# Attention with a SwiGLU gate on one core: projection steps in the issue table, rows by a task list, last phase by query blocks

## The chip, the core and the metric

The kernel runs on one core of a Trainium2 chip. The metric is the time of one execution on the device, in microseconds; a kernel's figure is the median of its runs.

## What is computed

x is 2048 x 512. It is layer-normalised, goes through full softmax attention with 32 heads of 16 columns and an output projection, and through a SwiGLU feed-forward of width 1792 whose result, passed through silu, scales the attention output. All of it is fp32.

```python
qkv = xn @ wqkv                       # S=2048, D=512, H=32, Dh=16
p = softmax(q @ k.T * Dh ** -0.5)     # per head
s = (p @ v).reshape(S, D) @ wo
h = silu(xn @ w1) * (xn @ w3)
g = silu(h @ w2)
return x + s * g
```

## The kernel before

Products that need fp32 accuracy run in the fp32r format with each operand split into a high and a low part; `split3` does a product as three matmuls (low x high, high x low, high x high). The values product is a plain fp32 matmul.

A prologue normalises x, transposes it, makes the values (`vt`, with a column of ones behind each head's 16), and writes q and k to DRAM. Then 32 *phases* run: 16 pairs of heads (`p`), each with the queries in two halves of 1024 (`half`). A phase has three kinds of steps:

- 64 *maxima* (m): a 62-row matmul of queries by keys into a PSUM bank (L482), whose row maxima DVE takes (L484). After the 64, `max_rows` makes them negative, transposes them (L496) and writes them by four small DMAs (L507) into two rows of the phase's `qs` tile, so that the scores come out with the maximum subtracted.
- 64 *scores* (s): keys by queries with 64 rows (L514); ACT takes the exponential into a `pt` tile (L517; there are 13).
- 16 *value blocks* (v): for a chunk of 128 keys, four fp32 matmuls of `vt` and four `pt` tiles (two heads, two blocks of 512 queries) side by side into one accumulator, `pv` (L524). The ones give the sums of the exponentials.

After the last value block of a phase `take_out` copies `pv` to `ot` (L530), writes the sums by DMA to a narrow tile (L536), takes 16-column reciprocals (L538), goes through DRAM to spread them over the rows (L540, L543), multiplies (L545), splits on POOL (L548, L549) and writes eight row pieces, `o<-oh` and `o<-ol` (L557), to DRAM. For the last pair, half 0, they go straight into the projection's tiles.

Beside the phases runs the feed-forward (f, L737), in blocks of 512 tokens in the order 3, 0, 1, 2, each in two halves of the width; its result g goes to DRAM, block by block. Weights arrive by DMA in `wr` and POOL splits them (L285, L286).

Scores, maxima and feed-forward matmuls use 64 of PE's 128 rows. Two such steps run at a time, one in each half, which the code calls lanes. The order in which everything is issued on PE is a string, `ORDER_OF_ISSUE`: f, m and s are steps of the lower lane, F, M and S of the upper, v is a value block, R the second part of `max_rows` (r: that and a value block), a dot an idle slot of the planner. A small planner (`Model`, with planned times of the lanes, ACT, DVE, POOL and DMA) runs along while the instructions are emitted. It decides which PSUM bank is taken and when the small steps of `max_rows` and `take_out` are put in; a step that can't go yet by its plan is put in `late` and emitted at the next place where it can. On the chip each engine and each DMA queue runs its instructions in the order of emission, held by semaphores.

The string covers 488 of the 512 value blocks. For the rest, a loop chooses steps by the planner's state. The output projection has 16 tiles of 128 tokens x 512, each twelve matmuls (`project`, lines L187, L189, L191 with the tile named `o`), and a `finish` on DVE: times g, plus x (L783, L785). It needs the attention rows (`ov`, fetched by L821), the output weights (L832, split on DVE at L825 and L826) and x and g (`bring`, L775, L776). All these DMAs are issued on SP, the fetches and `bring` from `open_chunk` at fixed chunk counts after the feed-forward's end. The loop takes six projection matmuls at a time when a counter (`beside["due"]`) says so.

Tokens of blocks 2 and 3 get their projection without the last two heads; these follow after the last value block. The closing chain there copies `pv`, transposes it, takes reciprocals, spreads and transposes back, multiplies, splits, and does a small projection of 64 rows for each tile of blocks 2 and 3 with a `finish` each (L1083 to L1114).

Of the kernel before, what the change touches and what calls it, by code (L numbers as in the profile page):

```python
# [26 lines left out]
VW = DH + 1  # L27
ORDER = (3, 0, 1, 2)
# [4 lines left out]
FEND = 3  # L33
RATE = 6
SPARE = 12
# [11 lines left out]
    "mMmMmMmM.fMffMffMffMffMffMfM.fMfm.Mm.MffFFffFfFFfFffFfFfFmFFmFffMfMfMffFFfFffFFmFfFfmFFmFmfFFffMfMfm"  # L47
    "MffMfmFfFfFfFFmFfFfmFFmFmFFfMffMfFffFFfFffFFmFfFfmMmFFmfFFmm.Mmf.MffMffFFfFffFFfFmFmFfFmfFFfFffMm.Mm"
    "MmFFffFfFfFfFfFfFfFfFmFfFfMfMfMmMmFfFfFfFfFFffFfFFffFFRFfMffMMfmFFfFfmFFmFfmFFfFmFfFfmFmMffSfMfmFfFf"
    "FfFfFFffFFffFFmfFSfmFfMfSffMfSfFfFfFmFsFmFfFsFmMfFsFfFfFfMfMfSfMfMfsFFffFFsFmFfmFmFSfFfFmFmvsMfMsFvv"  # L50
    "mSfSFfmSFffFsMfFsFmFsFFfMfSffSmFFffSmFfMvSmsMFmvFsMsMfFsfFFfMfsFfFMfSsfFMffMFfsFMfFfsFmFmSvvmSFsmFsF"
    "mFvSmfFSmfSFffMSffFmSfFmFsFfFmFSfSfmMvsMsMsMvsMMsfSMfvsMfMfSfMfMfSMfrvsMMffMfSfSffSfMsFffFsFFmsFfSmF"
    "fFfSmFmFFfSmvsMsMvvMsFffSFfmFFsSfmFfFfSfMfFFsFmfFSsmFvSsMffMsMvSmSfsFfMfFFfsMfFsFMfSffFMsfFFsmFfSFfm"
    "MvSmmMvSmmFsFFfFfsFmFSfFsmFfFfSMfFmFfmSvsMSmMfMfvSfmMMsvvSmfFsFfFFsMfmSfFsFfFmFfSMfFfmSvsMmSmFvSmmFF"
    "sfSfFfFMsfFMfMfsFFfMsfFfSfFsFMfsFfMSfmRvSmmSMmvvSfMffSfFsMFfsFmFsFFfmFsFmFmFsFFffSfMFfmSFfmFsFFfFmsF"
    "mFmFvSmmFsSvvMffSMffSfSFfMffSFfmSFfsFmFsFFfmFsFsFmFMfvvSmsSmMvsMSsFmFmvSmsFmFFmFsSsvmSfMSffSFffMsFFf"
    "sMfFMfSfMffFmSfFMmvSmmSmFvsFmFFmFsFsFmfFFsFffMfSSfMfSfFfMfMffFMmvsMMfMsvvSmSmFfmFfFFsmFFsSffFmFMfsFM"
    "ffSfFsFsFMfmrsMmSfMMfvsSfMmSvmSmMMsvsFfFSfmFSfFfMsFfSfMffSfFmFsFFmsFMffFFmMfSmvvMfSsFsFmfFfFmFsFfFmS"
    "fFSfMfsFfFsMfFMfMfsFvSsmSsSvvmSMfMsvSfMsFffFfSmFfSFsFmfFfFFsfSMffFFsfFMfFmmMvvSmfFFsmFFsFfMsFfFsmFSf"
    "FfmSFfSfSfMfFfmMFfvsMmSsSvvMsfMvMsSmSffFFfFfFsFmFfFsFmfSMfSffFmFSffFfMFmvvsMfSMfSffFfFfSMfsFMfFsFfFm"  # L60
    "sFFsFsmFFsFRvmSfSfMfMvsMSmmSvFmSmsSmFvSmsFmFfSfFfFFmfFsSMffFSffMFfMfMfsFfFsSvvMsMfsFsFFfFfFmFsFsFmSf"
    "FfmFmFFfmSvSmSssMvvmSMffSfSfMfMfSfSffMsMfFfsFsFfFmFmFMsvsMfMfSfFSffFmFsFMfmFmFvSmSmFmvSsmFMmvsMfSfMF"
    "fsFfFfMsFFfmSFfFsmFfSfFMmfFSffMvsMMfsSvsMsMMfvvsMfMfSSffSfMfMfMsrsMfMSfFffSFfMfSffMFfsFFsmFmFvvmSSfm"
    "SFfFfFfmFsFFfmSfFsFMfSfFfMsfFFmfFsFFfsSvsMSmmFvvSffMSfMfSffFfMsFsFFmmFFfSffMfFSmvsMsFmFsFfFFmsFFfMsf"
    "FsFMfsFFfmSFfMfSfmFvvSfSmSsMfvMsfMMfvSmmFsFsFFfFfMsfFsFMfsFfFSmFfFmSffFmFmSvSmsFsFmFFffFMsFfmFSfMfFf"
    "MsvvSsSfMfMffSfMvsMMmSrSmFssFFsFmmFvmSmFFsFffSFfmSmFSfFmfFsFFmFfFsFmFsFmfFfSFmSmvvSmSfSffMfSvMfsSfSm"
    "FFfFfFsFmFfFsMfsFfFsMfFsFMfMfFfmMvSmMfMmvvSmfSsFmFFfFfSmFfFsFmfFFsFmsFFmMfvsMMsSmvSmfSMffMfMfSMfvSfM"
    "ffMfMSffMfFFsFfFfsFmFmSFfFfsFsFMfsFFmMvMsmFsSvSmmSmMvsMSmvSmSffMfFsFFfMsfFSfSfFfMfMffSfFFsFmFmsFsFmF"
    "rMsFmmMFsvsMSmmFvSmSmFffFSfFfSfMfsFfFMfSfMfSffFFmFmmSmvvmFsFFssFFmFfMfsFFfmFsFmFfFSfMfMfSfmSvSmMsSsv"
    "sMSfMfMfMfvSmmMvSmsFfFFsFmFfsFMfFfsFMfFsfMFsfFMffMSffMMfvSmmSvSmSmmFvmMsFsFFsFfFfsFmFFfmSfFSffFmSfFS"  # L70
    "fMfMffFsSvMsSfMmvsMMfmFfFFsfFfSmFfFSfFmfSFmFfsFmFmFvMsmMMsvvsMfSMffSMfrSmfMSfsFfFFmsFFfMsfFFsMffMFfs"
    "FfMMfsFfFfFsSvMsSsmFmFvSmMsSmvfMfSmSfFfFfSmFsFfFMfSffFmSfFFsfFMfFfmMvvSsfSmMvmSFfsMsFFffSMfFfsFmFsFf"
    "FmFsFFfMfSfSfmMvsMMmmFvvSmFssFmFfFFfsFMfFsfMsFFfSfmSfsMffFfFmSfSfFmMvvmSmSvmSfFsFFmFsFfFmsFfMSfFfSfm"
    "FSffFMsfFMfsFMfvsMsMMsvsMSfSffMMffMfMrvsMfSfMMffSfMfSfSffSfFmFFfFmFsFmFfsMFfMsvSmmSFmvvMsFfFfFsSmFfF"
    "sFsfFMfFffSmFSffFSfMfFsFfSsvvmSSmSmvSmFmsFsFFmFsFmFmFsFmvsMmFsFFsFfFfMsfFSfMfSffFmFFsfMfFSffMfMfFFsM"
    "mvSsMsfSvmMSmMfvvSmSfSfMffSfMfMvsMfSmMFffFfFsFfFSsfFmFFsfFsFmFFfmMvsMsFfSfMfFfFmSFfSfMfSfFfmSFffFmFs"
    "FfMRvsMmMsSvvSmSffMvMsSmmFfFFffFSfFsFmFfsFFsFmfFSfmFFsfFmFFsmFFmSfFfFmFmSfvSmmMSmvmFFsFssMvSssMmFFmv"
    "vSfMffSfSMffFSfmFsFFfsMfFsFMfMfFfmMvvmMSffMFffSfFfSfMfSfMFfsMfFfMsFFmFFsFmmFFsFFsvMsmFmSSvSmSmmSvSmF"
    "ssFmFfFFfMsfFFsMffFFsMsFfMfMfvMsSfMfsSvMsMfMsfMvSffSMfSfmFFsFfFmsFFfmSfFsFFmmFFfFmSfSfRvSmsMMmvvSfMf"
# [61 lines left out]
def kernel(ctx: ExitStack, tc: tile.TileContext, x, wqkv, wo, w1, w3, w2, out):  # L141
# [1000 lines left out]
```

## Time and profile before

| | |
|---|---|
| time, median of 3 runs | 1836.4 us (1832.53 to 1837.69) |
| profiled execution | 1835.77 us, span 1834.0 us |
| granted TensorE clock, mean | 0.985 |
| PE busy | 1785.8 us (97%), 13120 matmul records |
| DVE busy | 1478.9 us (81%) |
| ACT busy | 1241.7 us (68%) |
| POOL busy | 692.0 us (38%) |
| DMA | 147.27 MB, mean 80 GB/s |

PE is the engine that matmuls run on, PEld its weight loads, which overlap. PE is counted as busy while a started matmul waits or runs at a low clock, so 97% does not say how near it is to its best. Times in the profile count from the start of the span. A line of the timeline has a start, a length, the engine, the line, the output and input tiles; in brackets, how long the engine was idle before it and what ended that. SPq is the queue of SP.

### The profile page before, as it was taken

The numbers are of one execution on the slowest core, as the hardware profiler recorded it, in microseconds if no ns is written. First come the engines' busy times: TensorE is split into PE (matmuls) and PEld (weight loads), VectorE is DVE, ScalarE is ACT, GpSimd is POOL, SyncE is SP. The second block draws the span as 40 slices with busy tenths as digits, with TensorE's granted clock in tenths as the row PEclk, the third lists the DMA queues.
The fourth block names the chain that finished last, engine by engine and source line by source line (L and its number), as shares of the span: only waits on it lengthen the run. The fifth ranks groups of instructions, "written<-read, shape, count | busy, mean of one in ns | idle before, by whom it ended". The sixth has DMA issues, their size and how long they took to land.

```text
span 1834.0 us, 35315 instructions
## 1 busy us (share of the span) xinstructions
PE 1785.8 (97%) x13120; PEld 1046.2 (57%) x13120; DVE 1478.9 (81%) x2450; ACT 1241.7 (68%) x2357; POOL 692.0 (38%) x720
## 2 busy tenths in 40 slices
PE   7999999999999999999999999999999999999896
PEld 5887655555555555555555555555555555554435
DVE  6425989988899888888888888998888898888415
ACT  3221477777777777777777776877777777777370
POOL 2104832455145514553345414560545235430001
PEclk9999999999999999999999999999999999999898
DMA  6656112122231303122312122132312131201823
GB/s 229 224 176 171 56 41 51 51 55 66 82 85 48 76 25 77 53 60 92 85 47 64 47 48 55 44 76 75 93 48 65 36 77 39 62 16 48 264 67 138
DMA packets 130203, 147.27 MB, mean 80 GB/s; under 512 B 28016, under 2 KB 86384, under 8 KB 126960
## 3 DMA queue, kind: packets, MB, share of 16 engines
q1 hardware_dynamic: 129456, 143.98, 28.6%
q8 instruction: 103, 1.69, 0.4%
q10 hardware_dynamic: 576, 1.05, 0.2%
q14 instruction: 68, 0.56, 0.1%
HBM read 104.33 MB, written 39.58 MB: 78 GB/s over the span
## 4 chain that ended last, share of the span: by engine, by line
PE 87%; DVE 5%; DMA 5%; SPq 1%; issue 1%; POOL 0%; ACT 0%; POOLq 0%; DVEq 0%
PE pv L524 25%; PE f L737 24%; PE e L514 17%; PE m L482 13%; DVE mp L484 4%; PE e L187 1%; PE e L191 1%; PE e L189 1%; DMA qk<-sl 1%; DMA ovl<-o 1%; PE o L187 1%; PE o L189 1%; PE o L191 1%; PE m L187 1%; PE m L191 1%
## 5 line engine op out<-in xcount | busy, mean ns | idle before, releaser
L484 DVE TENSOR_REDUCE mp<-m 128x1 f32<-128x512 f32 x2048 | 1297.6, 685 | 179.7 <-PE m L482 94.4
L517 ACT ACTIVATE pt<-e 128x512 f32<-128x512 f32 x2048 | 1085.5, 615 | 344.3 <-PE m L482 172.6
L482 PE MATMUL m<-ks,qs 62*128 62x512 f32 x2048 | 729.2, 421 | 10.0 <-DVE mp L484 4.9
L514 PE MATMUL e<-qs,ks 64*128 64x512 f32 x2048 | 728.3, 421 | 10.5 <-DVE mp L484 6.7
L524 PE MATMUL pv<-pt,vt 128*17 128x512 f32 x4096 | 523.8, 601 | 0.0
L514 PEld LDWEIGHTS e<-qs,ks 64*128 64x128 f32 x2048 | 343.3, 186 | 300.3 <-ACT pt L517 121.1
L482 PEld LDWEIGHTS m<-ks,qs 62*128 62x128 f32 x2048 | 347.2, 186 | 161.7 <-DVE mp L484 56.4
L737 PE MATMUL f<-xth,wl 64*128 64x512 f32 x896 | 312.5, 398 | 0.8 <-POOL wl L286 0.6
L737 PE MATMUL f<-xth,wh 64*128 64x512 f32 x896 | 309.6, 394 | 0.0
L737 PE MATMUL f<-xtl,wh 64*128 64x512 f32 x896 | 304.7, 394 | 0.0
L737 PE MATMUL f<-wh,hs 64*128 64x512 f32 x896 | 256.3, 394 | 0.0
L286 POOL TENSOR_TENSOR wl<-wr,wh 128x512 fp32r<-128x512 f32 x168 | 217.3, 1293 | 14.0
L285 POOL TENSOR_SCALAR wh<-wr 128x512 fp32r<-128x512 f32 x168 | 104.3, 621 | 260.4 <-DMA wr<-in_B_w_dram 71.5
L524 PEld LDWEIGHTS pv<-pt,vt 128*17 128x17 f32 x4096 | 80.2, 96 | 191.8 <-issue 182.5
L737 PEld LDWEIGHTS f<-xth,wl 64*128 64x128 f32 x896 | 154.8, 186 | 16.2 <-issue 2.1
L737 PEld LDWEIGHTS f<-xth,wh 64*128 64x128 f32 x896 | 156.4, 186 | 11.3
L737 PEld LDWEIGHTS f<-xtl,wh 64*128 64x128 f32 x896 | 153.4, 186 | 11.1
L737 PE MATMUL f<-wl,hs 64*128 64x512 f32 x448 | 156.3, 393 | 0.0
L737 PEld LDWEIGHTS f<-wh,hs 64*128 64x128 f32 x896 | 147.2, 185 | 11.3 <-issue 0.9
L548 POOL TENSOR_SCALAR oh<-ot 128x512 fp32r<-128x512 f32 x31 | 19.3, 621 | 319.5 <-DVE ot L545 319.5
L623 POOL TENSOR_TENSOR h<-g,h 128x512 f32<-128x512 f32 x56 | 72.0, 1285 | 176.0 <-ACT h L619 175.9
L607 POOL TENSOR_SCALAR th<-th 128x512 f32<-128x512 f32 x56 | 34.8, 621 | 156.5 <-ACT th L600 156.5
(112 smaller groups left out, 1219.6 us busy)
## 6 DMA issues: line engine op xcount, KB each, us to landing
wr<-in_B_w_dram SPq DMA_DIRECT2D x168, 256.0 KB
qs<-qk SPq DMA_DIRECT2D x192, 64.0 KB
ks<-qk SPq DMA_DIRECT2D x96, 128.0 KB
qk<-sh SPq DMA_DIRECT2D x32, 256.0 KB
qk<-sl SPq DMA_DIRECT2D x32, 256.0 KB
xin<-in_A_x_dram SPq DMA_DIRECT2D x16, 256.0 KB
g<-part SPq DMA_DIRECT2D x16, 256.0 KB
rb<-rd SPq DMA_DIRECT2D x124, 32.0 KB
```

What stands on the lines that cost most here:

```text
L187: nc.tensor.matmul(ps, lhs[1], rhs[0], start=first, stop=False)
L189: nc.tensor.matmul(ps, lhs[0], rhs[1], start=False, stop=False)
L191: nc.tensor.matmul(ps, lhs[0], rhs[0], start=False, stop=last)
L285: nc.gpsimd.tensor_scalar(hi, t, 1.0, 1.0, op0=ALU.mult, op1=ALU.mult)
L286: nc.gpsimd.tensor_sub(lo, t, raw(hi))
L482: nc.tensor.matmul(ps, qs[p % 2][64 * h:64 * h + KM, q0:q0 + P], ks[p % 2][64 * h:64 * h + KM, c * 512:(c + 1) * 512], start=True, stop=True)
L484: nc.vector.reduce_max(mp[p, half][:, h, qt, c:c + 1], ps, axis=AX.X)
L514: nc.tensor.matmul(ps, ks[p % 2][64 * h:64 * h + KR, k * P:(k + 1) * P], qs[p % 2][64 * h:64 * h + KR, q0:q0 + 512], start=True, stop=True)
L517: nc.scalar.activation(pt, ps, AF.Exp, scale=DH ** -0.5)
L524: nc.tensor.matmul(pv[32 * j:32 * j + VW, :], vt[:, k, 2 * p + j % 2, :], pt, start=(k == 0), stop=(k == NT - 1))
L623: nc.gpsimd.tensor_mul(h2, g, h2)
L737: nc.tensor.matmul(ps, left[r], right[r], start=starts and lane == 0, stop=ends and lane == 1)
```

## The change

The string is replaced by one that covers all 512 value blocks and has 21 letters o, one for each projection step; an o that can't go by the plan goes to `late`. Its other letters are re-laid too. It ends with:

```
old  ...RvvSsSssMvMsMffMfMSffMfSvvmFSmmSFmSmFFsFsFFmFsFsFmFFsFsSsFFmFmFmFFmFmFSvSmSsvSsSmSvSsSmSvMmSssSvSmsMsMvMsMsMvvM
new  ...FSvSsSsSvvMsMsMsSvMsSsSsvMsSsSovsSSssSovsSSsvmSsSSvvvRSssSsSovsSSsSsovsSsSSsovsSsSsSvSsSvosSSsSsvvsSsSsovvSsSsSos
     SsooovSssSsSoovSsSvvvoooooSsSsosSsSooSssSsvsSSvvv....
```

A step o is a whole tile of twelve matmuls at once (order of the blocks: 3, 2, 0), then "sum", then four "last" tiles of block 2, then block 1. The last phase takes its two blocks of 512 queries in turn, all 16 key chunks for block 2 and then for block 3. A value block then holds two key chunks of two heads, so block 2's sums, reciprocals and last product are done while block 3 is being attended; only block 3's are left for the closing chain. The sums are picked and spread by one matmul with a 0/1 matrix (`picks`), and the reciprocal is taken of all 512 columns.

`open_chunk` no longer starts transfers. A list of tasks, each with a condition, is gone through at each letter (`tend`): rows (r), output weights (wr), their split (w, on POOL now), side rows x and g (s), for blocks 3, 2, 0, 1. Nothing is started while the planned DMA work reaches over 3 us ahead. Block 3's rows and the output weights may come before the feed-forward's end. Side rows of block 0 go into the tiles of block 3's rows, those of block 1 into block 2's.

The first part of `max_rows` is put in as soon as its maxima are emitted.

```diff
+        if (p, half) == LAST:
+            qb, k = divmod(k * 2 + qb, NT)
...
-    def values(p, k, pts):
+    def values(p, half, k, pts):
+
+        last = (p, half) == LAST
         for j, pt in enumerate(pts):
-            nc.tensor.matmul(pv[32 * j:32 * j + VW, :], vt[:, k, 2 * p + j % 2, :], pt,
-                             start=(k == 0), stop=(k == NT - 1))
+            key = k * 2 % NT + j // 2 if last else k
+            nc.tensor.matmul(pv[32 * j:32 * j + VW, :], vt[:, key, 2 * p + j % 2, :], pt,
+                             start=key < 2 if last else k == 0, stop=key >= NT - 2 if last else k == NT - 1)
...
+    def split_rows(hi, lo, w):
+        nc.gpsimd.tensor_scalar(hi, w, 1.0, 1.0, op0=ALU.mult, op1=ALU.mult)
+        nc.gpsimd.tensor_sub(lo, w, raw(hi))
...
+    def bring(b):
+
+        if b == 3:
+            xs = [w_raw().rearrange("p a b -> p (a b)") for _ in range(4)]
+            gs = [raw(qs[NP % 2])[:, i * 512:(i + 1) * 512] for i in range(4)]
+        elif b == 2:
+            xs = parts_of(tail.tile([P, KC, 512], F32, name="x2"))
+            gs = [raw(w_split("hl"[i % 2])) for i in range(4)]
+        else:
+            pool, tag = (keep, "xt{}") if b == 0 else (tail, "ov{}2")
+            xs, gs = (parts_of(pool.tile([P, KC, 512], F32, tag=tag.format(v), name=f"in{v}{b}", bufs=1)) for v in "hl")
+        for t in range(4):
+            r = b * 512 + t * P
+            nc.sync.dma_start(xs[t], x[r:r + P, :])
+            nc.sync.dma_start(gs[t], g_d[b][t * P:(t + 1) * P, :])
+            side[b, t] = xs[t], gs[t]
...
+    def weights_split():
+        return wts.split == len(wts.units)
+
+    def attended():
+        return count["S"] >= 64 * (PHASES - 2)
+
+    tasks = [
+        ("r3", lambda: len(lanes.ended) >= 18 * TB * HF - 4, lambda: rows_of(3, by_rows(xt_pair(keep))), 0.0),
+        *(("r3", lambda: 3 in ov, lambda k=k: fetch(3, k), 2.5) for k in range(KC - 1)),
+        ("wr", weights_split, load_output_weights, 5.0),
+        *(("w", lambda: 3 in ov and to_split and attended() and mod.free["pool"] <= mod.now + 0.5,
+           lambda k=k: split_output_weights(k), 0.0) for k in range(KC)),
+        ("s3", lambda: attended() and len(wos) == 2 and len(wos[1]) == KC, lambda: bring(3), 9.0),
+        ("r3", lambda: 3 in ov and taken_out(PHASES - 3), lambda: fetch(3, 3), 2.0),
+        ("open", lambda: state["n"] >= UNITS and not owed, open_tail, 0.0),
+        *(("r2", lambda: tail, lambda k=k: fetch(2, k), 2.5) for k in range(KC - 1)),
+        ("r2", lambda: tail and taken_out(PHASES - 3), lambda: fetch(2, 3), 2.0),
+        ("s2", lambda: tail and len(wos) == 2 and len(wos[1]) == KC, lambda: bring(2), 9.0),
+        *(("r0", lambda: tail, lambda k=k: fetch(0, k), 2.5) for k in range(KC - 1)),
+        ("r0", lambda: tail and taken_out(PHASES - 4), lambda: fetch(0, 3), 2.0),
+        ("r1", lambda: tail and (2, 0) in side, lambda: rows_of(1, [[w_split(v) for _ in range(KC)] for v in "hl"]), 0.0),
+        *(("r1", lambda: 1 in ov, lambda k=k: fetch(1, k), 2.5) for k in range(KC)),
+        ("wl", lambda: 1 in ov, last_rows, 1.0),
+        ("s0", lambda: gone(3), lambda: bring(0), 9.0),
+        ("s1", lambda: gone(2), lambda: bring(1), 9.0),
+    ]
+
+    def tend():
+
+        while tasks and mod.free["dma"] <= mod.now + 3.0:
+            e = next((e for e in tasks if e[1]()), None)
+            if e is None:
+                return
+            tasks.remove(e)
+            e[2]()
+            if e[3]:
+                there[e[0]] = mod.work("dma", mod.now, e[3]) + 2.5
+
+    def got(*names):
+        return not any(e[0] in names for e in tasks) and all(there.get(n, 0.0) <= mod.now for n in names)
+
+
+    steps = [("whole", b, t) for b in (3, 2, 0) for t in range(4)]
+    steps += [("sum", 2, 0)] + [("last", 2, t) for t in range(4)] + [("whole", 1, t) for t in range(4)]
+
+    def can(what, b):
+        if what == "sum":
+            return len(sums) == 2 and sums[1] <= mod.now
+        if what == "last":
+            return len(sums) == 3 and sums[2] <= mod.now and got("wl")
+        return got("w", f"r{b}", f"s{b}") and (b >= TB // 2 or taken_out(PHASES - 2))
...
+    def finish(b, t, i, ps, to, adder=None):
+
+        xr, gr = side[b, t]
+        res = tail.tile([P, 512], F32, tag="res", name="res", bufs=2) if adder is None else pt_tile(F32)
+        nc.vector.scalar_tensor_tensor(res, gr, 0.25, ps, op0=ALU.mult, op1=ALU.mult)
+        (adder or nc.vector).tensor_add(xr, res, xr)
+        free_at[i] = mod.work("dve", max(mod.lane) + 0.25, 1.4) - 0.7
+        if to is not None:
+            r = b * 512 + t * P
+            to.dma_start(out[r:r + P, :], xr)
...
+        if not steps or min(free_at) > mod.now + EARLY or not can(*steps[0][:2]):
+            return False
+        what, b, t = steps.pop(0)
+        i, ps = take("o")
+        if what == "sum":
+            mod.block(4, was_free[i])
+            ot = sums[0]
+            nc.tensor.matmul(ps, picks(), ot, start=True, stop=True)
+            oh, ol = (work.tile([P, 512], F32R, tag=f"o{v}", name=f"o{v}", bufs=1) for v in "hl")
+            nc.vector.reciprocal(rb, ps)
+            nc.vector.tensor_mul(ot, ot, rb)
+            nc.vector.tensor_scalar(oh, ot, 1.0, 1.0, op0=ALU.mult, op1=ALU.mult)
+            nc.vector.tensor_sub(ol, ot, raw(oh))
+            free_at[i] = mod.work("dve", max(mod.lane) + 0.25, 2.0) - 1.2
+            sums.append(free_at[i] + 2.2)
+            side["split"] = oh, ol
+            return True
+        if what == "whole":
+            mod.block(3 * KC, was_free[i])
+            for k in range(KC):
+                run(split3(ps, [v[k][:, t * P:(t + 1) * P] for v in ov[b]], [w[k] for w in wos], k == 0, k == KC - 1))
+        else:
+            mod.block(3, was_free[i])
+            run(split3(ps, [v[:, t * P:(t + 1) * P] for v in side["split"]], wlast, True, True))
+        finish(b, t, i, ps, nc.sync if b < TB // 2 or what == "last" else None)
...
+    def picks():
+
+        if not chosen:
+            m = work.tile([P, P], F32, tag="mh", name="picks", bufs=2)
+            for j in range(4):
+                of = [ident[:, n:n + 1].to_broadcast([P, 32]) for n in (32 * (j % 2) + DH, 32 * (j % 2) + 64 + DH)]
+                nc.vector.tensor_add(m[:, 32 * j:32 * j + 32], *of)
+            chosen.append(m)
+        return chosen[0]
...
-        if tail is None and state["n"] >= UNITS and not owed:
-            open_tail()
-            end = count["chunks"]
-        n = count["chunks"] - end
-        if tail:
-            if n == 1:
-                output_weights()
-                mod.work("dma", mod.now, 4.0)
...
-        if tail and count["V"] < PHASES * NT:
-            beside["due"] = min(beside["due"] + max(beside["left"] - SPARE, 0) / (PHASES * NT - count["V"]), 5 * RATE)
-        if k == NT - 1 and (p, half) != (NP - 1, 1):
+        if (p, half) == LAST:
+            if k == NT // 2 - 1:
+                sums.append(work.tile([P, 512], F32, tag="ot", name="ot", bufs=1))
+                nc.scalar.copy(sums[0], pv)
+                pv_free = mod.work("act", begins + mod.VALUES + 0.3, 0.6) + mod.NOTICE
+                sums.append(pv_free)
+        elif k == NT - 1:
...
-    while count["V"] < PHASES * NT:
+    while count["V"] < PHASES * NT or len(steps) > 1:
         settle()
         small()
-        catch_up()
+        tend()
         if rows and rows[0][2] == 1 and rows[0][0] <= mod.now:
             second()
-        if values_ready(mod.now) and (len(closed) > 1 or not exponentials(0) or not exponentials(1)):
-            issue_v()
-            continue
...
         if values_ready(mod.now):
             issue_v()
...
+        elif not any(half_issued(what, h) for h in sorted(range(2), key=lambda h: mod.lane[h]) for what in "smf"):
+            if not projecting():
+                mod.wait(0.1)
+
+    ot, oh, ol = pt_tile(F32), pt_tile(F32R), pt_tile(F32R)
     nc.scalar.copy(ot, pv)
-    while beside["left"]:
+    while steps:
+        settle()
+        small()
+        tend()
         mod.wait(0.1)
-        small()
         projecting()
-    turned, back = bank("o"), bank("o")
-    for c in range(4):
-        nc.tensor.transpose(turned[:, c * P:(c + 1) * P], ot[:, c * P:(c + 1) * P], ident)
...
+    total = bank("o")
+    for c in (slice(0, 256), slice(256, 512)):
+        nc.tensor.matmul(total[:, c], picks(), ot[:, c], start=True, stop=True)
+    for c in (slice(0, 256), slice(256, 512)):
+        nc.vector.reciprocal(rb[:, c], total[:, c])
+        nc.vector.tensor_mul(ot[:, c], ot[:, c], rb[:, c])
+        nc.vector.tensor_scalar(oh[:, c], ot[:, c], 1.0, 1.0, op0=ALU.mult, op1=ALU.mult)
+        nc.vector.tensor_sub(ol[:, c], ot[:, c], raw(oh[:, c]))
     for t in range(4):
```

More of the change, by code (lines that the diff above doesn't have):

```diff
@@ L27 @@
 VW = DH + 1
+LAST = (NP - 1, 1)
 ORDER = (3, 0, 1, 2)
@@ L836, in output_weights, with split_output_weights, last_rows @@
+    def split_output_weights(k):
+        if not wos:
+            wos.append([raw(ks[NP % 2]).bitcast(F32R)[:, i * 512:(i + 1) * 512] for i in range(KC)])
+            wos.append([])
+        wos[1].append(w_split("hl"[k % 2]))
+        split_rows(wos[0][k], wos[1][k], to_split[k])
+    wlast = []
+    def last_rows():
+        w = tail.tile([P, 512], F32, tag="res", name="res", bufs=2)
         nc.gpsimd.memset(w, 0.0)
@@ L1094 @@
-    spread = tail.tile([P, 512], F32, tag="res", name="res", bufs=2)
-    nc.vector.tensor_copy(spread.rearrange("p (a b) -> p a b", b=32),
-                          rec.rearrange("p (a b) -> p a b", b=1).to_broadcast([P, 16, 32]))
-    for c in range(4):
-        nc.tensor.transpose(back[:, c * P:(c + 1) * P], spread[:, c * P:(c + 1) * P], ident)
-    nc.vector.tensor_mul(ot, ot, back)
-    oh = work.tile([P, 512], F32R, tag="oh", name="oh", bufs=1)
-    ol = work.tile([P, 512], F32R, tag="ol", name="ol", bufs=1)
```

355 lines of the change are left out of this document (136 added, 219 removed).

## The prediction

> **What bounds the kernel now.** I read the busy time by stretches first, with cuts where the character of the work changes: end of the prologue, last feed-forward matmul, first score of the last phase, last value block, last full projection. Columns are length, then busy time of PE, weight load, DVE, ACT, POOL, then granted clock, DMA share and GB/s.
>
> ```profile
> 161.00:1686.60 1525.60, 1515.89 (x11858) 862.64 (x11860) 1350.55 (x2233) 1138.34 (x2161) 657.56 (x674) 1.00 0.24 59
> 1686.60:1746.60 60.00, 50.34 (x244) 23.13 (x245) 29.97 (x53) 27.60 (x55) 4.50 (x7) 0.85 0.70 224
> 1746.60:1780.50 33.90, 33.88 (x198) 11.24 (x199) 2.07 (x3) 31.08 (x63) 1.91 (x2) 0.91 0.12 33
> 1780.50:1813.20 32.70, 32.70 (x144) 26.99 (x145) 15.18 (x22) 0.59 (x1) 0.00 (x0) 1.00 0.50 175
> 1813.20:1834.00 20.80, 5.60 (x33) 3.96 (x31) 13.13 (x19) 0.00 (x0) 5.06 (x4) 0.69 0.32 122
> ```
>
> The first stretch is TensorE at full clock with 9.7 us idle in 1525.6 (1525.60 less 1515.89): nothing but the amount of matmul work counts there. The other four are the tail, 147.4 us, and each has another limit. The first of them holds 244 matmul records in 60 us, where 32.7 us of the fourth hold 144: PE is busy there only because matmuls wait. The chain of waits, cut to the tail, says for what (start, length, piece):
>
> ```profile
> 1692.42 2.87 DMA wr<-in_A_wo_dram
> 1701.47 5.06 DMA ovl<-o
> 1724.11 6.61 DMA wl<-g
> 1730.74 6.56 DMA wl<-o
> 1737.32 3.37 DMA sums<-ot
> 1744.72 1.75 DMA qs<-ml
> ```
>
> From 1692 to 1746 it is a row of transfers: the output weights, attention rows and side rows queued together on SP, and behind them the 2 KB sums and the maxima rows `qs<-ml` that the last phase's scores need. The third stretch is paced by ACT, with projections hardly beside it; the fourth is 12 projection tiles with ACT empty; the fifth is the closing chain. So work of three limits runs in turn, and could in part run side by side. The timeline gives the unit prices and two of the stalls:
>
> ```profile
> 1684.88 0.40 PE L737 MATMUL f<-wh,hs 64*128 64x512 f32 x1
> 1702.43 0.79 PE L514 MATMUL e<-qs,ks 64*128 64x512 f32 x1 [5.97 <-DVE mp L484]
> 1700.00:1705.00 5.00, 2.57 (x12) 0.90 (x16) 4.34 (x8) 1.19 (x2) 0.65 (x2) 0.50 0.88 298
> 1745.26 0.47 PE L514 MATMUL e<-qs,ks 64*128 64x512 f32 x1 [2.52 <-DMA qs<-ml]
> 1753.80 0.66 PE e L514 x4
> 1754.46 0.98 PE pv L524 x8
> 1757.69 19.34 ACT L517 ACTIVATE pt<-e 128x512 f32<-128x512 f32 x39
> 1791.44 0.39 PE L187 MATMUL o<-ks,xtl 128*128 128x512 f32 x1
> 1802.32 0.39 PE L187 MATMUL o<-ks,wl 128*128 128x512 f32 x1
> ```
>
> The last feed-forward matmul ends at 1685.3. Four scores cost PE 0.66 us and a value block 0.98 us where ACT doesn't hold them; an exponential costs ACT 19.34/39 = 0.496 us, so a chunk takes 1.64 us of PE and 1.98 of ACT. A projection matmul takes (1802.32 - 1791.44)/48 = 0.2267 us, a tile of twelve 2.72 us. A wait of 5.97 us left the clock at 0.50 in the stretch 1700 to 1705.
>
> **The body of the table.** The whole string is replaced, so I counted it. Up to value block 450 the old one has 3780 f, 1896 m and 1803 s letters, the new one 3779, 1895 and 1809; adding the larger of the two lanes between value blocks gives 3774 slots against 3780. The work is the same and in the same proportions, so I take no change. Bounds: the 9.7 us of idle could vanish or double, so 9.7 us either way. Up to the last f, the new string has 24 slots (24 x 0.2267 = 5.4 us) and 3 value blocks (3 x 0.98 = 2.9 us) more. They are no extra work, they are only done before that mark: it moves from 1685.3 to 1693.6.
>
> **After the last f.** The string still has 105 scores, 29 value blocks, 6 maxima and all 21 projection steps. On PE: scores 105/4 x 0.66 = 17.3; value blocks 29 x 0.98 = 28.4; maxima 3 slots, 0.7; 16 whole tiles x 2.72 = 43.5; four "last" tiles x 3 x 0.2267 = 2.7; the new sum, one fp32 matmul of 512 columns, about 1.0 by the fp32 value block (0.5 to 2). Sum 93.6 us. ACT needs 105 x 0.496 = 52.1 us beside it, so with projections between the chunks ACT no longer sets the pace. That takes the third stretch's pacing and the fourth stretch's solo run away; what it costs if that cover fails is 0.34 us (1.98 - 1.64) for each chunk without projection beside it, 8 us for 24.
>
> **Transfers.** Bytes stay the same (rows, side rows, weights, 4 MB of output). What moves is their order: rows of block 3 and the output weights come about four down-products before the last f, where the DMA share was low; the rest in batches, each held back until the planned queue is short. The weights' split goes from DVE to POOL, with these prices, four times:
>
> ```profile
> L286 POOL TENSOR_TENSOR wl<-wr,wh 128x512 fp32r<-128x512 f32 x168 | 217.3, 1293 | 14.0
> L285 POOL TENSOR_SCALAR wh<-wr 128x512 fp32r<-128x512 f32 x168 | 104.3, 621 | 260.4 <-DMA wr<-in_B_w_dram 71.5
> ```
>
> 4 x 1.9 = 7.7 us on POOL, which was busy 4.50 of 60 us there; DVE is rid of the block that made the 5.97 us wait. I cost it at nothing; if POOL were late the first projection would wait, up to those 7.7 us.
>
> Each projection now stands in PE's in-order queue at a fixed place. If its rows are late, every score and value block behind it waits too, and ACT and DVE with them. Three places matter, priced by the following rows:
>
> ```profile
> 1631.64 0.59 ACT L530 COPY ot<-pv 128x512 f32<-128x512 f32 x1 [1.80 <-PE pv L524]
> 1656.14 0.42 SPq L557 DMA_DIRECT2D o<-ol  x1
> 1742.55 0.70 SPq L507 DMA_DIRECT2D qs<-mh  x1
> 1746.62 3.21 PE e L514 x9
> SPq L775 <- PE o L191: 29.7, 2, 20.4
> ```
>
> An output of a phase takes 1656.14 - 1631.64 = 24.5 us from the copy to the last row write, plus landing, about 2 us (`qs<-ml` above: 1.75). (1) The first tile needs phase 29's rows; from value block 480 to the first o the string has 44 slots and 8 value blocks, 18 us. Late by 0 to 9; I take 3, since a step that can't go yet is put behind later chunks. (2) The last phase's maxima rows: 4 us from issue to use (1742.55 to 1746.62), behind a transpose and two casts of about 1.2; between it and the last phase's first score stand 8 scores, one tile and one value block, 5.0 us. With side rows queued ahead, one stream of 5.06 us more. 0 to 6, I take 3. (3) Block 0 needs phase 30's rows, written straight into its tiles: 26 us, against seven value blocks (6.9), 35 scores (5.8) and four tiles (10.9), 23.6 us. Late by 2; with block 1's side rows in front, another stream or two: 0 to 12, I take 5. The clock after such waits, by the 0.50 row, about 2. Together 13 us, 2 to 29.
>
> **The closing chain.** Before, it took 20.8 us (fifth stretch). Two rounds of transposes go; one matmul picks the sums, the reciprocal runs over 512 columns instead of 16, in halves.
>
> ```profile
> 1733.93 0.17 DVE L492 TENSOR_SCALAR nm<-mx 128x16 f32<-128x16 f32 x1
> 1814.74 0.25 DVE L1092 RECIPROCAL rec<-o 128x16 f32<-128x16 f32 x1
> 1780.65 0.59 ACT L1083 COPY ot<-pv 128x512 f32<-128x512 f32 x1 [1.66 <-issue]
> 1816.27 0.69 DVE L1099 TENSOR_TENSOR ot<-ot,o 128x512 f32<-128x512 f32 x1 [0.82 <-PE o L1098]
> 1816.99 0.43 DVE L1102 TENSOR_SCALAR oh<-ot 128x512 fp32r<-128x512 f32 x1
> 1819.88 0.69 DVE L783 SCALAR_TENSOR_TENSOR res<-qs,o 128x512 f32<-128x512 f32 x1 [1.73 <-PE o L191]
> 1822.52 1.27 DVE L785 TENSOR_TENSOR wr<-res,wr 128x512 f32<-128x512 f32 x1
> 1830.73 0.34 ACTq L788 DMA_DIRECT2D out_dram<-wl  x1
> ```
>
> Copy with its wait 0.8, first half of the matmul 0.5, four DVE steps over 512 columns 0.69 + 0.69 + 0.43 + 0.69 = 2.5, DVE's four products and two additions 6 x 0.69 = 4.1, one addition slowed beside POOL (1.27) 0.6, first products on PE 0.7, last issue to the end of the span 3.3 (1834.0 - 1830.73): 12.5 us. Block 2's product and half of the additions are already gone, which is where 8 us go. The reciprocal is the unknown: at the multiply's rate it is 0.69; by the two 16-column rows it costs (0.25 - 0.17)/16 = 5 ns a column more, 2.6 us over 512. I take 0.69, as part of the 0.08 us may be a fixed cost; the other end adds 2.6 us at the close, and a little at the first sum, which has value blocks behind it.
>
> **Sum.** 1693.6 + 93.6 + 13 + 12.5 = 1812.7 us of span, 21.3 less than 1834.0. The profiled execution took 1835.77, 1.8 us around its span, so 1814.5; the median of the runs is 1836.4, 0.6 higher. Forecast 1814.5 us.
>
> **The rivals.** *Everything hides.* The waits come down to 2 us: 1803.5. For it: the tail's bytes, 224 x 60 + 33 x 34 + 175 x 33 + 122 x 21 = 23 MB by the stretches, take 77 us at the 298 GB/s of 1700 to 1705, and there are 119. Against: the output chain's 24.5 us is a row, not a guess. Chance 0.17.
> *The steps don't land between the chunks.* The late list pushes most of them behind the last phase: chunks run at ACT's pace (8 us), no wait vanishes: 1822.5, with a slow reciprocal 1825. For it: only 18 to 24 us of work cover chains of 26. Against: every chunk put ahead of a late step shortens its wait. Chance 0.13.
> *A slow wide reciprocal.* At 5 ns a column the close is 2.6 us longer: 1817.1. For it the 16-column rows, against it that they can't part a fixed cost from one a column. Chance 0.15.
> The Trainium skill, "VectorE: DVE Perf Modes", section "Walkthrough: the 8-slice pipeline in each mode", says that the reciprocal is an iterated divide with a repeat count of 8. Taken as eight passes a column, an estimate from that page is 5.5 us instead of 0.69, and the time would be 4.8 us longer than forecast; no run here shows a wide reciprocal.
> *SP holds up the table (slower).* Side rows of block 0 and 1 go into tiles that projections of block 3 and 2 read; SP stands at them until PE is through, and what is queued behind stands with it: the writes of phase 30's rows. Such stands took 29.7 us in before, the longest 20.4. They cost nothing there, as PE had other work; now PE itself waits for those rows with everything queued behind. With 29.7 us on top of 13 the time is 1844. It decides once PE's waits after the last f pass 40 us (13 + 1841.9 - 1814.5). Against: SP's hold ends when PE reaches the tile, and these tiles stand before block 0 in PE's queue. Chance 0.12.
>
> **How the numbers follow.** About 0.3%, 5.5 us, is what a measurement of this kernel can tell from no change: faster is below 1830.9, slower above 1841.9. The forecast case, 1806 to 1822, has 0.40; with the first three rivals faster has 0.85. 0.03 stays for a gain eaten by the body's 9.7 us, 0.12 for slower. The range reaches from 1796 (the first rival with some of the body's idle gone) to 1834 (the steps behind the last phase, the body's 9.7 us on top, 1832, and most of a slow reciprocal); about 0.05 lies below and 0.15 above.
>
> **What would show it.** Right: the last f near 1694; no DMA run of 50 us in the chain of waits; ACT's exponentials with projection matmuls between them; no stretch of 12 tiles alone after the last value block; 12 to 13 us from there to the end; largest PE waits at the first tile of block 0, behind `o<-` or row writes. Wrong: the last f off by more than 5 us (the body is then not the same); PE waits over 40 us after it; a reciprocal of 512 columns over 2 us; matmul records in the body stretch at the same count but with more than 20 us idle.

## The result, and the profile after

The changed kernel takes 1837.3 us (median of 12 runs, 1832.3 to 1840.1), the kernel before, on the same chip, 1836.6 (12 runs, 1832.0 to 1839.6). The ratio is 1.0005, with a 95% interval of 0.9994 to 1.0017: no change. The forecast was 1814.5 with a range of 1796 to 1834, so the prediction was wrong. The profiled execution took 1838.15 us and its span is 1836.4.

Busy time by stretches of the changed kernel, cut here at the last feed-forward matmul, the first projection matmul, the step of the sums and the last value block. Columns: length, then busy time of PE, weight load, DVE, ACT and POOL, then clock, DMA share, GB/s.

```profile
161.00:1711.90 1550.90, 1531.98 (x11906) 864.99 (x11906) 1358.29 (x2254) 1149.77 (x2171) 666.04 (x684) 0.99 0.25 61
1711.90:1728.70 16.80, 16.80 (x112) 5.47 (x111) 7.28 (x13) 16.16 (x34) 2.88 (x4) 1.00 0.41 140
1728.70:1781.00 52.30, 49.32 (x265) 26.66 (x264) 12.36 (x20) 29.11 (x58) 4.31 (x5) 0.97 0.67 217
1781.00:1820.50 39.50, 36.53 (x176) 22.00 (x176) 21.76 (x32) 9.84 (x19) 0.00 (x0) 0.96 0.22 81
1820.50:1836.40 15.90, 6.30 (x17) 3.76 (x16) 10.16 (x14) 0.58 (x1) 2.51 (x2) 0.68 0.18 66
```

The last four stretches, the tail, are 124.5 us (1836.4 less 1711.9). Before they were 148.7 (1834.0 less 1685.3). So the tail did get shorter by 24.2 us, of which 8.3, by the forecast's count, is work now done before the mark. But the mark itself, the last feed-forward matmul, moved from 1685.3 to 1711.9, which is 26.6 us. The body lost what the tail won. Of the row of transfers in the chain that ended last, two are left behind the mark, one after the other:

```profile
1772.02 4.35 DMA inl<-g
1776.38 4.44 DMA ovl<-ol
```

The twelve tiles that ran alone behind the last value block are gone too: the last stretch holds 17 matmul records. The first stretch now has 18.9 us of idle PE (1550.9 less 1531.98) where it had 9.7, and its clock is 0.99.

The waits of PE and DVE from 161 to 1710 us say which idle that is (total, times, longest). Of the changed kernel:

```profile
DVE rec L552 <- DMA sums<-ot: 19.1, 6, 7.4
PE m L491 <- DVE mp L493: 11.4, 7, 6.3
PE e L525 <- DVE mp L493: 4.4, 4, 2.7
```

Of the kernel before, the first two of these rows:

```profile
DVE rec L538 <- DMA sums<-ot: 7.8, 5, 2.1
PE m L482 <- DVE mp L484: 4.9, 6, 1.8
```

(The third row is 6.7 us there, but 6.0 of it is the stop at 1702 us, behind the mark.)

One of the worst places, in the timeline of the changed kernel (start, length, line; in brackets the idle time before and what ended it). The key rows (L328), five `wr` loads (L282), the query rows (L337) and the sums of an output (L550) are all issued from SP, in the order of the lines; the sums are read from `ot`, which ACT copies:

```profile
505.42 2.64 SPq L328 DMA_DIRECT2D ks<-qk  x6
508.11 8.21 SPq L282 DMA_DIRECT2D wr<-in_B_w_dram  x5
...
516.92 2.75 SPq L337 DMA_DIRECT2D qs<-qk  x6
519.77 2.47 SPq L550 DMA_DIRECT2D sums<-ot  x4
...
509.90 0.59 ACT L544 COPY ot<-pv 128x512 f32<-128x512 f32 x1
...
513.49 2.65 DVE L493 TENSOR_REDUCE mp<-m 128x1 f32<-128x512 f32 x4 [0.55 <-PE m L491]
523.58 0.25 DVE L552 RECIPROCAL rec<-sums 128x16 f32<-128x16 f32 x1 [7.43 <-DMA sums<-ot]
...
524.43 0.79 PE L491 MATMUL m<-ks,qs 62*128 62x512 f32 x1 [6.29 <-DVE mp L493]
```

The same place in PE's windows of 5 us (busy time, count, clock, DMA share, GB/s):

```profile
520.00:525.00 5.00, 0.57 (x2) 0.75 0.15 39
525.00:530.00 5.00, 5.00 (x25) 0.57 0.29 82
530.00:535.00 5.00, 5.00 (x44) 1.00 0.00 0
```

`ot` is there at 510.5. But SP is at the weight loads until 516.3, of which it stands 5.5 us before the last of the five, and sends the sums only at 519.8. The reciprocal of 16 columns, 0.25 us of work, stands at the head of DVE's queue for 7.43 us. The maxima `mp` behind it can't run, so their banks don't come free, and PE stops for 6.29 us. Then PE runs 5 us at a clock of 0.57: 25 matmuls where the next 5 us hold 44. Two more such places lie at 720 and 1305 us, with reciprocals that stood 3.16 and 5.63 us. PE's windows of 50 us around the three places, where an undisturbed 50 us holds some 396 matmul records:

```profile
500.00:550.00 50.00, 43.71 (x327) 0.93 0.38 86
700.00:750.00 50.00, 47.09 (x348) 0.93 0.36 69
1300.00:1350.00 50.00, 46.14 (x344) 0.93 0.38 91
```

That makes the count of matmul records in a fixed stretch a good measure of the body. From 161 to 1650 us, PE's row of the windows, of the kernel before and then of the changed one:

```profile
161.00:1650.00 1489.00, 1479.50 (x11578) 1.00 0.24 60
```

```profile
161.00:1650.00 1489.00, 1470.47 (x11442) 0.99 0.25 61
```

The changed kernel is 136 matmuls behind. At the rate of before (11578 in 1489 us, 7.8 a us) that is 17.5 us, of which 9.0 are idle time (18.5 against 9.5). Up to the mark the work is as counted: 11906 records from 161 us on against 11848.

### The profile page after: what moved, and what is told of

Same layout as the page of the kernel before. It is cut to its first block, busy times and chain, and to the rows that moved or that the text cites. A ratio compares the mean times of both kernels' runs of the same rounds, so it can differ in the third digit from the quotient of the medians.

```text
span 1836.4 us, 35395 instructions
## 1 busy us (share of the span) xinstructions
PE 1787.7 (97%) x13118; PEld 1040.8 (57%) x13118; DVE 1478.3 (81%) x2453; ACT 1249.5 (68%) x2358; POOL 699.4 (38%) x728
## 4 chain that ended last, share of the span: by engine, by line
PE 88%; DVE 7%; DMA 3%; SPq 1%; POOL 1%; issue 1%; ACT 0%; DVEq 0%; POOLq 0%; ACTq 0%
PE pv L538 26%; PE f L751 24%; PE e L525 17%; PE m L491 13%; DVE mp L493 5%; PE e L186 1%; PE e L190 1%; PE e L188 1%; PE o L186 1%; PE o L190 1%; PE o L188 1%; SPq L337 1%; PE m L186 1%; PE m L190 1%; PE m L188 1%; DMA wr<-in_B_w_dram 1%
## 5 line engine op out<-in xcount | busy, mean ns | idle before, releaser
L491 PE MATMUL m<-ks,qs 62*128 62x512 f32 x2048 | 719.8, 420 | 15.7 <-DVE mp L493 11.4
L751 PE MATMUL f<-xtl,wh 64*128 64x512 f32 x896 | 311.4, 396 | 0.0
L751 PE MATMUL f<-wh,hs 64*128 64x512 f32 x896 | 262.1, 396 | 0.0
L562 POOL TENSOR_SCALAR oh<-ot 128x512 fp32r<-128x512 f32 x31 | 19.1, 617 | 266.4 <-DVE ot L559 244.9
```

The costliest lines, as they stand in the source:

```text
L491: nc.tensor.matmul(ps, qs[p % 2][64 * h:64 * h + KM, q0:q0 + P], ks[p % 2][64 * h:64 * h + KM, c * 512:(c + 1) * 512], start=True, stop=True)
L751: nc.tensor.matmul(ps, left[r], right[r], start=starts and lane == 0, stop=ends and lane == 1)
```

## The experiments

The change has two parts: a new string (everything up to the last phase reordered), and new code and string for the tail. The first four runs separate them, and try the waits. Each ratio is to the kernel before, run beside it on the same chip (medians 1834.3 us in experiments 1 and 2, 1835.8 in 3 and 4, 1837.0 in 5). "String to 400" is the letters up to the 400th value block, which hold none of the tail's steps.

**1. Halves exchanged.** `a_old400` is the changed kernel with the old string to 400. `b_new400` is the kernel before with the new string to 400. The whole edit is in the table of letters.

> The changed kernel with the old string up to value block 400 and the new one behind it (two m made M, five s and S added, so that the counts agree). Both theories: the body gives back what it lost, the last feed-forward matmul at 1691 to 1696 instead of 1702, time 1826 to 1831, and the waits for sums come down to about the 7.8 us of before. If the tail alone is to blame, time stays at 1837.

> The kernel before with the new string up to value block 400 (counts made to agree the other way). Body to blame: slower by 6 to 11 us, 1842 to 1847, with the three long waits for sums near 520, 722 and 1305 us. Tail alone to blame: 1836.5.

Measured: `a_old400` 1823.6, ratio 0.9944 [0.9930, 0.9958]; `b_new400` 1850.4, ratio 1.0085 [1.0072, 1.0098]. The new tail gains with either first part (0.56% with the old one, 0.80% with the new: 10 and 15 us), and the new first part loses in either code (0.85% and 0.61%: 16 and 11 us). So the two effects cancel, and the loss goes with the letters, not with the new fetching of rows: the old code with the new letters has holes in the same windows (331, 374 and 340 matmuls) and the same wait:

```profile
DVE rec L538 <- DMA sums<-ot: 18.9, 6, 7.7
```

The sizes missed: `a_old400` is faster than expected and `b_new400` slower, and the waits for sums in `a_old400` came down to 12.0 us, not to 7.8; its mark is at 1701.2, not at 1691 to 1696. The 1702 in the expectations of this experiment and the next is not the mark of the changed kernel's trace, which is 1711.9.

**2. The reciprocal planned later.** In both kernels, for the outputs of phases 0 to 27. The steps of an output behind the reciprocal move back with it:

```
-                c[0] = mod.now + 3.5
+                c[0] = mod.now + (8.0 if c[3] == 0 and c[2] < 28 else 3.5)
+                c[3] += 1
```

> The changed kernel; only the 16-column reciprocal of phases 0 to 27 is put in 8.0 instead of 3.5 us of planned time behind the DMAs of its sums. Theory 1 (DVE stands at that reciprocal until the sums have landed, 19.1 us in the profile of the changed kernel, and PE stands behind the maxima): DVE's wait for the sums falls under 4 us, the last feed-forward matmul moves from 1702 to 1684..1690, time 1820 to 1826. Theory 2 (the new string is slower by its own order, the waits for sums are only where it shows): the last feed-forward matmul stays within 4 us of 1702, time 1833 to 1838.

> The kernel before with the same edit for the same phases. Theory 1: its 7.8 us of waits for sums go, 1829 to 1834, so less is gained than in the changed kernel. Theory 2: no change, 1835 to 1838.

Measured: the changed kernel 1825.5, 0.9949 [0.9936, 0.9962]; the kernel before 1824.9, 0.9944 [0.9932, 0.9957]. The changed kernel's mark moved from 1711.9 to 1699.5, less far than theory 1 had it, and the time is in its range. The old kernel gained more than expected. Its own two thin windows (369 matmuls from 900, 365 from 1100 us) went to 395 and 397: it had been losing to such waits too, only less. In one of them DVE had stood 2.1 us at the reciprocal (1105 us), in the other 1.4 us at the product behind it, which waits for a DMA of its own (913 us); the edit moves both. In the changed kernel 6.7 us of standing were left (expected under 4), near 520 and 1310 us, so 8.0 was not enough there.

**3. The sums off SP's queue.** Their DMAs are issued from ACT (`nc.sync` to `nc.scalar` at L550).

> The changed kernel with the four DMAs of each phase's sums issued on ACT's queue, right behind the copy, instead of SP's; the reciprocal stays 3.5 us of planned time behind. Theory 1 (SP is what makes the sums late): DVE's wait for the sums under 3 us, last feed-forward matmul at 1693 to 1700, time 1818 to 1828, although ACT issues 124 DMAs more. Rival (the DMA engines or the landing are slow, whatever the queue): the waits stay above 10 us, time 1832 or more.

Measured: 1860.2, 1.0131 [1.0116, 1.0145], slower, against both theories. Two waits of PE, and one each of DVE and ACT, in the body (its last f ends at 1735.4 us):

```profile
PE e L525 <- ACT pt L528: 16.0, 14, 1.7
PE m L491 <- ACT pt L528: 11.8, 9, 1.9
...
DVE rec L552 <- DMA sums<-ot: 3.9, 2, 2.2
...
ACT pt L528 <- DMA sums<-ot: 28.3, 15, 2.7
```

DVE's standing fell from 19.1 to 3.9 us, and PE's two waits for the maxima from 15.8 to 3.6, so SP's queue was what made the sums late. But ACT now stands itself, 28.3 us at its exponentials where it issues the sums, and PE waits 27.8 us for ACT. The same four DMAs cost more in the queue of an engine that computes. Why the sums were late is confirmed; as a cure this is worse than the fault.

**4. Slack everywhere, and two costs of the tail.** For phases 0 to 27, `a_slack` plans the reciprocal at 12.0 and the product at 8.0 us behind what they wait for (3.5 for both in the changed kernel), and builds the masks `picks` early, when the tail is opened. On top of it, `a_slack_norecip` puts copies for the wide reciprocals (L932, L1155), so the last phase is not divided by its sums, and `a_slack_norow29` reads the third chunk of rows twice for blocks 3 and 2 and does not fetch the fourth.

> The changed kernel with, for phases 0 to 27, the reciprocal 12.0 and the product with rb 8.0 instead of 3.5 us of planned time behind the step before, and the picks matrix built when the tail is opened. Theory 1: nothing is left of DVE's waits for sums and rb in these phases, the last feed-forward matmul lands at 1692 to 1696, as the count of letters has it; PE's 2.0 us wait for picks goes too; 1815 to 1820. If the body has another loss of its own, the last feed-forward matmul stays at 1698 or later and the time above 1822.

> As a_slack, but the two wide reciprocals (512 columns at the sum, twice 256 at the close) are plain copies, so the last phase's output is not divided by its sums. Theory (each sits on the path: 3.36 + 2 x 1.76 us measured, against 0.4 to 0.7 for a copy of as many columns): 4 to 5.5 us less than a_slack. Rival (the first has value blocks behind it): only the close counts, 2.5 us less.

> As a_slack, but the projection of blocks 3 and 2 reads its third chunk of rows a second time in place of the fourth, and the fourth, which waits for phase 29's rows, is not fetched (768 KB less). Theory 2 (the first projection tile waits for phase 29's output chain, and until then PE goes at ACT's pace): the first tile starts at least 10 us earlier, 3 to 6 us less than a_slack. Rival (later waits, block 0's rows and the sum, set the end): the same time within 1.5 us.

Measured: `a_slack` 1826.1, 0.9946 [0.9934, 0.9959]; without reciprocals 1821.2, 0.9915 [0.9898, 0.9932]; without the fourth chunk 1825.4, 0.9942 [0.9925, 0.9958]. The wide reciprocals cost 4.9 us of the time. The fourth chunk's wait costs nothing that can be told: the first projection came 7.6 us earlier (1710.6 instead of 1718.2), and the time moved by 0.7. No reciprocal stood in `a_slack`, yet its last feed-forward matmul came at 1701 and the time at 1826, which the expectation had taken for a sign of another loss in the body. Its timeline shows one thing that took the place:

```profile
639.84 0.62 POOL L562 TENSOR_SCALAR oh<-ot 128x512 fp32r<-128x512 f32 x1 [1.52 <-DVE ot L559]
...
647.63 1.29 POOL L637 TENSOR_TENSOR h<-g,h 128x512 f32<-128x512 f32 x1
...
649.70 1.26 POOL L639 TENSOR_TENSOR hs<-h,hs 128x512 fp32r<-128x512 f32 x1
...
651.02 0.65 PE L751 MATMUL f<-wh,hs 64*128 64x512 f32 x1 [2.00 <-POOL hs L639]
```

POOL waits for the product `ot` and splits it, then does three weight blocks, and only then the feed-forward's hidden block that PE needs. PE stops 2.0 us, and the clock of 650 to 660 is 0.83. That is one place, and not the whole of the loss. So whether the new string was also slower by its own order was still open.

**5. Only the wait, taken out of both codes.** `a_rec12` is the changed kernel with 12.0 instead of 8.0 in the edit of experiment 2, `b_new400_rec12` the same in `b_new400`. `a_old400_later` is `a_old400` with 8.0 and early masks; `a_rec12_mul5` is `a_rec12` with the product at 5.5 and early masks.

> The changed kernel with the 16-column reciprocal planned 12.0 us behind its transfers of the sums (3.5 in the changed kernel, 8.0 in the run before) in all steps before the last phase; nothing else moved. At 1650 us the run with 8.0 had 104 matmuls less behind it than the old kernel with the same edit; 69 of them were missing in 500 to 550 and in 1300 to 1350 us, where its reciprocal still waited. Theory (the body's whole loss is such holes): they fill, 69 matmuls at 8 a us are 8.6 us, the last feed-forward matmul at 1689 to 1694 (1699.5 with 8.0), the time 1814 to 1820. Rival (the new string is slower by its own order, maxima beside scores): the last feed-forward matmul at 1697 or later, the time 1823 or more.

> The old kernel's code with the new string up to value block 400, and the reciprocal 12.0 planned us behind its sums. Without that edit it took 1850.4, its windows of 50 us from 500, 700 and 1300 us held 331, 374 and 340 matmuls where 396 is usual: 143 missing, 17.9 us. Theory (holes): they fill, 1832 to 1838, the last feed-forward matmul by 1686 (1700.1 without). Rival (own order of the new string): it gains 5 to 9 as the changed kernel did with 8.0, 1841 to 1846, the last feed-forward matmul at 1691 or later.

> The changed code with the old string up to value block 400 (1823.6 as it stood), the reciprocal 8.0 planned us behind its sums, and the masks of ones (picks) written when the last feed-forward matmul is through instead of at the sums that use them. Theory (holes and a shorter tail add up): the old string lost 10 us of waits by the same edit in the old kernel; here its holes (361 matmuls from 1100 to 1150, 382 from 450 to 500 us) are some 50 matmuls, 6 us, and the masks 2: 1812 to 1817, faster than both kernels. Rival (filling the body only moves the wait to the tail): 1820 or more.

> As the changed kernel with 12.0, with the product behind the reciprocal planned 5.5 us behind its row (3.5 in the changed kernel, 8.0 in the run with slack for both), and the masks written early. The run with 12.0 and 8.0 had no such wait left and yet ended its feed-forward at 1701: its windows held 382 and 373 matmuls from 600 to 700 us, where POOL split the late product ahead of the feed-forward's hidden block, which PE awaited for 2.0 us. Theory (8.0 pushed POOL's work together): with 5.5 that is gone, 1813 to 1819. Rival (own order): 1823 to 1827, as with 8.0.

| run | us | ratio, 95% interval | last f ends | after it | matmuls 161 to 1650 |
|---|---|---|---|---|---|
| before (profiled execution) | 1836.6 | | 1685.3 | 148.7 | 11578 |
| changed (profiled execution) | 1837.3 | 1.0005 [0.9994, 1.0017] | 1711.9 | 124.5 | 11442 |
| a_old400 | 1823.6 | 0.9944 [0.9930, 0.9958] | 1701.2 | 126.1 | 11526 |
| b_new400 | 1850.4 | 1.0085 [1.0072, 1.0098] | 1700.1 | 147.5 | 11457 |
| a_rec_later | 1825.5 | 0.9949 [0.9936, 0.9962] | 1699.5 | 123.0 | 11539 |
| b_rec_later | 1824.9 | 0.9944 [0.9932, 0.9957] | 1675.6 | 150.1 | 11650 |
| b_new400_rec12 | 1832.4 | 0.9975 [0.9965, 0.9985] | 1683.2 | 147.2 | 11592 |
| a_rec12 | 1818.5 | 0.9903 [0.9889, 0.9916] | 1692.0 | 123.8 | 11596 |
| a_old400_later | 1815.5 | 0.9881 [0.9867, 0.9894] | 1690.1 | 123.6 | 11608 |
| a_rec12_mul5 | 1826.3 | 0.9936 [0.9924, 0.9949] | 1700.7 | 124.5 | 11528 |

The last three columns are from the profiled execution of each. `a_rec12`, `b_new400_rec12` and `a_old400_later` came out in the ranges of the theory of the holes, and `a_old400_later` is the fastest version, faster than both kernels. The same place at 520 us in the timeline of `a_rec12`, and PE's windows of the three places:

```profile
508.97 8.55 SPq L282 DMA_DIRECT2D wr<-in_B_w_dram  x5
...
518.13 2.75 SPq L337 DMA_DIRECT2D qs<-qk  x6
520.98 3.38 SPq L550 DMA_DIRECT2D sums<-ot  x4
...
514.37 6.01 DVE L493 TENSOR_REDUCE mp<-m 128x1 f32<-128x512 f32 x9 [0.54 <-PE m L491]
522.03 3.77 DVE L493 TENSOR_REDUCE mp<-m 128x1 f32<-128x512 f32 x6 [1.66 <-PE e L525]
525.72 0.24 DVE L552 RECIPROCAL rec<-sums 128x16 f32<-128x16 f32 x1
```

```profile
500.00:550.00 50.00, 50.00 (x393) 1.00 0.39 86
700.00:750.00 50.00, 50.00 (x403) 1.00 0.40 81
1300.00:1350.00 50.00, 49.99 (x390) 1.00 0.23 63
```

SP's queue is the same and the sums leave as late as before. But the reciprocal no longer stands ahead of them: DVE does fifteen maxima meanwhile, PE doesn't stop, and the three windows hold 393, 403 and 390 matmuls (327, 348 and 344 without the edit). That is 167 matmuls more; from 161 to 1650 us it is 154 more, so the gain is these three places.

`a_rec12_mul5` missed: 1826.3 instead of 1813 to 1819. The longest single stop of PE in the body that grew is again for `hs` on POOL, near 450 us: 2.6 us, where `a_rec12` has 1.7. It shows the clock's share. PE's windows there, in `a_rec12` and then in `a_rec12_mul5`:

```profile
450.00:455.00 5.00, 4.12 (x31) 1.00 0.75 260
455.00:460.00 5.00, 5.00 (x44) 1.00 0.40 165
```

```profile
450.00:455.00 5.00, 2.37 (x20) 1.00 0.37 95
455.00:460.00 5.00, 5.00 (x29) 0.66 0.66 246
```

The wait of 1.7 us left the clock at full speed, the one of 2.6 us left 5 us at 0.66. From 450 to 500 this run has 357 matmuls where `a_rec12` has 393: 36, or 4.6 us. The other 32 of the 68 that it lacks by 1650 us are spread over the body; what stops PE there was not traced. The masks can't be the reason, as by the code they are built only when the last f is through; so it is the product, moved back by 2.0 us. The early masks bring nothing that shows: its tail is 124.5 us, that of `a_rec12` 123.8.

## Why the prediction was wrong, step by step

**The body of the table** is the step that failed. It said that the work is the same in the same proportions, "so I take no change", and put the mark at 1693.6. It came at 1711.9, 18.3 late. The counting of letters was right about PE's work (58 records more before the mark, 7.5 us at 7.8 a us, where 8.3 us was forecast), and the count is blind to the order in which SP's queue reaches the sums. With the reciprocal planned later the mark is at 1692.0 (`a_rec12`), and the time 1818.5. So what failed was the assumption that a small transfer in front of a 0.25 us instruction stays on time.

That 1692.0 is so near the forecast's 1693.6 is in part luck. The forecast started from the mark of before, 1685.3, and before lost to such waits too: with the edit it is at 1675.6 (`b_rec_later`). From there the forecast's 8.3 us give 1683.9, and `a_rec12` is 8.1 later. So of the 18.3 us, by the marks of single profiled executions, 10.2 are the wait beyond what before had of it, and 8.1 are a loss of the new string that no run here explains. The medians agree roughly: the new first part lost 16 us in the old code and 11 in the new, and with the waits gone 5.7 (0.9975 against 0.9944) and 4.0 (0.9903 against 0.9881, whose delay is 8.0 and whose masks are early).

**Its bounds** failed too. The idle of 9.7 us "could vanish or double", and it did double, to 18.9. But I let the idle stand for the whole loss. Most of the rest of what is missing is matmuls run at a lower clock behind each stop: 0.57 for 5 us at 525, and 0.93 over each of the three windows of 50 us, some 10 us in all, where the two thin windows of before had 0.97, some 3 us. I charged the clock for the tail's waits and not for the body's. The trace of before had the warning: its reciprocals stood five times, and two of its windows were 27 and 31 matmuls short of 396. I read "9.7 us idle in 1525.6" as nothing to be gained; `b_rec_later` gained 0.56%, 10 us, from it.

**After the last f:** forecast 93.6 of PE work and 13 of waits, 106.6 to the last value block; measured 108.6 (1820.5 less 1711.9). The sum held, its parts did not, so that its holding is luck. The waits were 6.0 us of idle (3.0 in each of the third and fourth stretches), and the waits of PE from 1711 us, here without those of the closing chain, have none at the rows of blocks 3 and 2:

```profile
PE pv L538 <- ACT ot L1066: 2.2, 1, 2.2
PE o L930 <- DVE picks L958: 2.0, 1, 2.0
PE o L186 <- DVE ol L935: 1.0, 1, 1.0
PE o L186 <- DMA ovl<-ol: 0.7, 1, 0.7
```

Place (1) cost nothing, as the first tile came 16.8 us behind the mark with value blocks ahead of it, and `a_slack_norow29` shows that getting it earlier brings nothing. Place (3), block 0's rows, was forecast at 5 and is the 0.7. Place (2) left no wait in the list. In return PE's work took longer, 102.6 us and not 93.6: the stretch before the first tile is paced by ACT (16.16 us busy of 16.80), so "ACT no longer sets the pace" holds only from there on, and the clock was 0.97 and 0.96 in the two stretches behind it. How the 9.0 us split was not measured. I had not placed a wait at the masks, which DVE only builds when the sums are asked for.

**The closing chain** was forecast at 12.5 and took 15.9 us. The term that was mis-sized is the reciprocal. In the timeline, 512 columns at the sums and the first 256 of the two halves at the close:

```profile
1793.99 3.36 DVE L932 RECIPROCAL rb<-o 128x512 f32<-128x512 f32 x1 [2.07 <-PE o L930]
...
1822.37 1.76 DVE L1155 RECIPROCAL rb<-o 128x256 f32<-128x256 f32 x1 [6.03 <-PE o L1153]
```

I took 0.69 us for 512 columns, the multiply's rate, and called the 16-column rows' 5 ns a column the other end. The two halves took 3.5 us, 2.8 more than forecast (most of the rest is the matmul in front of them, 1.15 us and not 0.5); the chance of 0.15 for the slow rival was too small, and its 2.6 us the better value. The Trainium skill, "VectorE: DVE Perf Modes", section "Walkthrough: the 8-slice pipeline in each mode", gives the divide a repeat count of 8. The estimate from it was 5.5 us for 512 columns, and the trace shows 3.36, so the direction agrees and the measurement decides the size.

**The rivals.** "SP holds up the table" had the mechanism, SP standing at a held load with row transfers behind it, but in the wrong place: I put it in the tail, by way of projections on PE, where the runs show nothing of it. It acted in the body, by way of DVE; I had priced only the stands at side rows, which "cost nothing" in before, and looked at none in the body. "Same" had a chance of 0.03, for "a gain eaten by the body's 9.7 us". That is what happened, at nearly twice the size. Of the 23.7 us by which the span missed its forecast, 18.3 lie before the mark, 2.0 between it and the last value block, and 3.4 in the closing chain.

**What stays open.** With the reciprocals' wait gone, the new first part is still slower than the old, by the 4 to 6 us above. `a_rec12` has 54 matmuls less by 1650 us than `b_rec_later`, 7 us. Its waits name 1.7 us at `hs` and 2.5 at a weight load, and not the rest. Nor is the cure free of chance: with the product moved too, the body lost 8 to 9 us again (`a_slack`, `a_rec12_mul5`).

## What to carry to other kernels

Counting work per engine tells what a reordered table needs, not what stands at the head of an in-order queue. For each small instruction that waits for a DMA, look up how long its engine stood there, and what SP had to issue first; a row like "reciprocal, 7.8 us in 5 waits" on an engine that feeds the busiest one is a warning before the change, and moving the instruction back a few microseconds is a cheap cure to try, one instruction at a time: here it paid for the reciprocal and cost as much again for the product. Measure a body by its matmul records in a fixed stretch: busy time hides what the clock takes after a stop.

## What the runs showed of the hardware

Three reciprocal sizes fit one line: 0.242 us for 16 columns, 1.754 for 256 and 3.356 for 512 are 6.3 ns a column and 0.15 us fixed. A copy in its place took 0.42 us for 256. A PE wait of 1.7 us left the clock at 1.00 in the next 5 us, one of 2.6 us left 0.66, one of 6.3 us 0.57. The length does not decide it alone: in the kernel before a wait of 1.6 us at 915 us left 0.66 too, with 26 matmuls in 5 us. And four small DMA issues took 3.19 us of ACT's queue, in which ACT stood idle 2.71 us (`a_sums_act`, timeline):

```profile
864.06 3.19 ACTq L550 DMA_DIRECT2D sums<-ot  x4
867.29 1.08 ACT L528 ACTIVATE pt<-e 128x512 f32<-128x512 f32 x2 [2.71 <-DMA sums<-ot]
```
